# A transformer block in float32: the MLP's down projection from seven block products instead of eight, tokens in two blocks of 1024

## The chip, the cores and the metric

One core of one Trainium2 chip runs the kernel. Its engines have queues of their own: TensorE (PE, with its weight loads shown apart as PEld), VectorE (DVE), ScalarE (ACT), GpSimd (POOL) and SyncE (SP), which here issues nearly all DMAs. TensorE writes its results to PSUM, from where another engine has to fetch them. The metric is the device time of one execution in microseconds. Before the change it is 1821.71 us, the median of 3 runs (1820.71 to 1821.91).

## The reference

```python
x = A_x                                         # 1 x 2048 x 576
mod = (silu(c) @ w_mod).reshape(1, 6, 1, -1)    # sa, ca, ga, sb, cb, gb
h = layernorm(x) * (1 + ca) + sa
x = x + ga * attention(h, wqkv, wo)             # 32 heads, window 256
h = layernorm(x) * (1 + cb) + sb
# block B on h:
g  = gelu(layernorm(h) @ w1)                    # four column groups shifted
x1 = h + shift(g) @ w2                          # by +1, -1, +2, -2 tokens
h2 = gelu(layernorm(x1) @ w3) @ w4              # w3: 576 x 4608, w4: 4608 x 576
x = x + gb * (x1 + h2)
```

All inputs and outputs are float32. The change is in the line of `h2`, the MLP: an up projection to 4608 features, gelu, and a down projection back to 576.

## The kernel before

Matrix products run in a reduced float32 format of TensorE. To keep precision, each operand is split into a high part (a copy rounded to that format, by ScalarE) and a low part (the rest, a subtraction on VectorE or GpSimd), and a product is the sum of three: high by high, high by low, low by high. `products` lists the 14 matmuls of a contraction over 576 (four chunks of 128 rows with three products each, and the 64 rows left over with their low parts stacked into two).

Phase A computes the attention, and phase B the layer norms and the first half of block B (w1, gelu, shifts, w2). Phase B leaves the transposed, split, normalised activations `LNT[g]` for four groups of 512 tokens, and writes `x1` (`accd`) and the residual `x` (`xp`) to DRAM.

Phase C is the MLP. It goes over 18 groups `fg` of 256 hidden features (`NF` = 2 chunks of 128), and within each over 4 token groups `tt` of 512. `up(fg, tt)` makes for each chunk a PSUM tile of 128 features by 512 tokens from 14 matmuls (L1111), applies gelu on ScalarE (L1115, into `gf`), and splits it into `Gc`: the high part on ScalarE (L1117), the low part on VectorE (L1118). `down(fg, tt)` makes for each of 4 token tiles and each half `hf` of 288 output columns a PSUM tile from 2 chunks x 3 = 6 matmuls (L1136) and adds it on VectorE to an accumulator in SBUF (L1140, L1138 for the first group). The 16 accumulators of 128 x 576 stay in SBUF through all 18 groups. The down projection of a unit comes one unit after its up projection.

`weights(fg)` loads two chunks of w3 and two of w4, multiplies w4 by `gb` on GpSimd (L1085), and splits both; the low parts are made on GpSimd, for the first group on VectorE (L857 and L858 for w3, L94 for w4). Raw rows go through a ring of 6 buffers (`row`), split weights through a ring of 9 (`wc`). Once per token tile, between groups 1 and 8, GpSimd computes `x1 * gb + x` and adds it to the accumulator (L1146 to L1148). In the last group each finished accumulator goes to the output by a DMA of 128 x 576.

The order: each step is an event with a time, and `play` runs the events in order of time, which gives the order of the source. In phase A all compute engines keep this order. In phases B and C a scheduler may move instructions on each engine, also across the border between the phases; so weight splits of phase C stand among the last instructions of phase B on GpSimd. PSUM holds, in these phases, tags `w1` (3 tiles, the up projection), `w2` and `tr` (2 each, the down projection) and `mm` (1).

## Time and profile before

| | |
|---|---|
| median of 3 runs | 1821.71 us |
| the profiled execution | 1821.39 us, span 1819.6 us, granted TensorE clock 0.991 |
| PE busy | 1745.1 us (96%) |
| DVE, ACT, POOL busy | 909.8, 631.9, 515.9 us |
| first and last start of an up matmul (L1111) | 892.6 and 1806.0 us |
| first and last start of a down matmul (L1136) | 909.5 and 1815.7 us |
| matmuls of the up and the down projection | 2016 of 128 x 512, 3456 of 128 x 288 |

The page of the profile gives each engine's busy time, the chain of work that ended last, followed back from the last instruction, and groups of instructions. Other views give the durations of the instructions of a line, the instructions in order of time, and busy times in chosen stretches. L12 is line 12 of the kernel before. Matmuls are pipelined: the ends of single ones are modelled, and the spacing of their starts is the better measure.

### The profile page before, as it was taken

To read this page: it belongs to the slowest core of one execution; us is meant where nothing else is said; L and a number is where in the kernel's file an instruction comes from. 1 tells how busy PE (TensorE), PEld (TensorE's weight loads), DVE (VectorE), ACT (ScalarE), POOL (GpSimd) and SP (SyncE) were. 2 spreads that over 40 slices of the span, in tenths; PEclk is the share of its full clock that TensorE was granted. 3 is DMA by queue.
4 is the path that set the end of the run, shared out by engine and by line. 5 is a ranking of instruction groups with operands and counts; after the bars stand their busy time and mean duration, and the time that the engine had idled before them with its cause. 6 is when DMAs were issued, how large, how long until landed. Compare 5 with 4: busy or idle time off the path is not lost.

```text
span 1819.6 us, 30069 instructions
## 1 busy us (share of the span) xinstructions
PE 1745.1 (96%) x11520; PEld 1488.1 (82%) x11520; DVE 909.8 (50%) x2467; ACT 631.9 (35%) x1169; POOL 515.9 (28%) x559
## 2 busy tenths in 40 slices
PE   8899999999998897999899999999999999999999
PEld 5767677777766674888899999999999999999998
DVE  4565665565565763667634443344443333443334
ACT  3354454454455554433222222222222222222211
POOL 7333332321134543112414432343312211221100
PEclk9999999999999998999999999999999999999999
DMA  7554453344356654433301110111101000110002
GB/s 212 163 159 144 122 163 119 114 130 115 89 139 184 194 173 133 143 105 109 123 16 54 47 50 26 54 54 54 53 17 42 26 24 22 28 28 7 1 1 105
DMA packets 128119, 161.18 MB, mean 89 GB/s; under 512 B 35044, under 2 KB 69860, under 8 KB 127976
## 3 DMA queue, kind: packets, MB, share of 16 engines
q1 hardware_dynamic: 127656, 158.74, 29.7%
q8 instruction: 91, 1.49, 0.3%
q10 hardware_dynamic: 320, 0.52, 0.1%
q14 instruction: 52, 0.43, 0.1%
HBM read 107.81 MB, written 50.73 MB: 87 GB/s over the span
## 4 chain that ended last, share of the span: by engine, by line
PE 82%; DVE 5%; POOL 4%; DMA 4%; ACT 2%; issue 2%; SPq 1%; ACTq 0%; POOLq 0%; DVEq 0%
PE p L1136 25%; PE p L1111 25%; PE qk L363 5%; PE av L532 4%; PE X L502 4%; PE sc L455 4%; PE v L363 2%; PE X L511 2%; PE pg L983 2%; PE po L750 2%; PE w L1034 2%; DMA wm<-in_w_mod_dram 1%; DVE sc L462 1%; POOL wm L581 1%; PE oT L543 1%
## 5 line engine op out<-in xcount | busy, mean ns | idle before, releaser
L1111 PE MATMUL p<-LNT,W 128*128 128x512 f32 x2016 | 482.8, 390 | 0.0
L1136 PEld LDWEIGHTS p<-W,Gc 128*128 128x128 f32 x3456 | 472.7, 188 | 11.1
L1136 PE MATMUL p<-W,Gc 128*128 128x288 f32 x3456 | 480.4, 295 | 0.0
L1111 PEld LDWEIGHTS p<-LNT,W 128*128 128x128 f32 x2016 | 371.5, 188 | 69.2
L462 DVE CUSTOM_DVE_ANT_0 sc<-sc,mask 128x384 f32<-128x384 f32 (+2 forms) x512 | 271.2, 541 | 201.1 <-PE sc L455 198.5
L1115 ACT ACTIVATE gfc<-p 128x512 f32<-128x512 f32 x144 | 86.0, 597 | 662.6 <-PE p L1111 662.6
L1140 DVE TENSOR_TENSOR accA<-p,accA 128x288 f32<-128x288 f32 x340 | 151.6, 453 | 316.8 <-PE p L1136 314.9
L521 ACT ACTIVATE P<-X 128x512 f32<-128x512 f32 (+2 forms) x384 | 216.7, 570 | 232.6 <-PE X L511 226.9
L455 PE MATMUL sc<-K,Q 108*128 108x384 f32 (+2 forms) x512 | 191.7, 382 | 5.8 <-DMA k0d<-qe 3.3
L1140 DVE TENSOR_TENSOR accB<-p,accB 128x288 f32<-128x288 f32 x204 | 92.5, 455 | 198.0 <-PE p L1136 196.1
L94 POOL TENSOR_TENSOR W<-r,W 128x576 fp32r<-128x576 f32 x34 | 48.6, 1429 | 466.0 <-ACT W L93 465.9
L502 PE MATMUL X<-Q,K 110*128 110x128 f32 (+2 forms) x704 | 163.0, 306 | 3.7 <-ACT P L521 3.4
L363 PE MATMUL qk<-hT,Wc 128*128 128x512 f32 x504 | 159.4, 414 | 3.6 <-ACT qe L384 1.4
L502 PEld LDWEIGHTS X<-Q,K 110*128 110x128 f32 x704 | 123.9, 191 | 28.7 <-issue 9.4
L1118 DVE TENSOR_TENSOR Gc<-gfc,Gc 128x512 fp32r<-128x512 f32 x144 | 117.5, 816 | 7.7 <-ACT Gc L1117 3.9
L511 PE MATMUL X<-maskb,identb 128*128 128x256 bf16 (+1 forms) x640 | 120.6, 254 | 0.0
L455 PEld LDWEIGHTS sc<-K,Q 108*128 108x128 f32 x512 | 97.5, 193 | 27.8 <-issue 11.7
L363 PEld LDWEIGHTS qk<-hT,Wc 128*128 128x128 f32 x504 | 86.2, 192 | 19.0 <-issue 5.1
L532 PE MATMUL av<-P,V 128*32 128x384 f32 (+2 forms) x1408 | 99.6, 394 | 0.0
L388 POOL CAST qe<-qe 128x512 fp32r<-128x512 f32 x36 | 22.2, 616 | 256.3 <-ACT qe L384 241.2
L1117 ACT CAST Gc<-gfc 128x512 fp32r<-128x512 f32 x144 | 89.3, 620 | 3.6
L363 PE MATMUL v<-Wv,hT 128*128 128x288 f32 x448 | 82.4, 306 | 3.8 <-ACT qe L384 2.9
(891 smaller groups left out, 1842.4 us busy)
## 6 DMA issues: line engine op xcount, KB each, us to landing
K<-k0d SPq DMA_DIRECT2D x96, 108.0 KB
r<-in_B_w_dram SPq DMA_DIRECT2D x36, 288.0 KB
Q<-q0d SPq DMA_DIRECT2D x128, 72.0 KB
K<-k1d SPq DMA_DIRECT2D x48, 108.0 KB
wm<-in_w_mod_dram SPq DMA_DIRECT2D x17, 288.0 KB
x<-in_A_x_dram SPq DMA_DIRECT2D x16, 288.0 KB
Q<-q1d SPq DMA_DIRECT2D x64, 72.0 KB
od<-o SPq DMA_DIRECT2D x32, 144.0 KB
```

Source lines behind the costliest of these rows:

```text
L363: nc.tensor.matmul(pm, pl()[i][0], pl()[i][1], start=(i == 0), stop=(i == 13))
L455: nc.tensor.matmul(sc[:, lo:], q[0:2 * R3, h, i * P:(i + 1) * P], k[0:2 * R3, h // 2, i * P + lo:(i + 3) * P], start=True, stop=True)
L462: nc.vector.tensor_tensor_reduce(out=sc[:, lo:], in0=sc[:, lo:], in1=mask[:, lo:], scale=1.0, scalar=-3e38, op0=ALU.add, op1=ALU.max, accu ...
L502: nc.tensor.matmul(x[:, p0 * P:(p0 + w) * P], k[0:2 * R3 + 2, h // 2, (kb + 2) * P:(kb + 3) * P], q[0:2 * R3 + 2, h, q0 * P:(q0 + w) * P], ...
L511: nc.tensor.matmul(x[:, p0 * P:(p0 + w) * P], self.identb, m, start=False, stop=(n == len(ms) - 1))
L521: nc.scalar.activation(pt[:, c0:c1, h % 2, :], x[:, c0 * P:c1 * P].rearrange("p (a b) -> p a b", b=P), AF.Exp, scale=SCALE)
L532: nc.tensor.matmul(abox[0][32 * h:32 * h + 32, q0 * P:(q0 + w) * P], v[:, hh * VA:hh * VA + 32], Pt[b, h // 2][:, p0:p0 + w, h % 2, :], st ...
L1111: nc.tensor.matmul(pg, w, a, start=(i == 0), stop=(i == len(pl) - 1))
L1117: nc.scalar.copy(Gh, gf)
L1118: nc.vector.tensor_tensor(out=Gl, in0=gf, in1=Gh.bitcast(F32), op=ALU.subtract)
L1136: nc.tensor.matmul(po, a, w, start=(i == 0), stop=(i == len(seq) - 1))
L1140: nc.vector.tensor_tensor(out=acc[t][:, cs], in0=po, in1=acc[t][:, cs], op=ALU.add)
```

## The change

The down projection of a unit is seen as a product of 2 x 2 blocks: 1024 tokens in two halves of 512 (`tt`), 256 features in two chunks of 128 (`j`), 576 columns in two halves of 288 (`DH2`). It is computed from seven products of blocks instead of eight (Winograd's form of Strassen's scheme): combinations of blocks of the gelu output and combinations of blocks of w4 are multiplied, and the products are kept in seven accumulators per token tile, which are combined after the last group.

- Tokens go in two blocks `blk` of 1024, so all of w3 and w4 is needed twice. In block 0 the weights are loaded, combined and split as before, and the split tiles are stored to DRAM (`w3d`, `w4d`); in block 1 they are loaded from there.
- A unit has 4 PSUM tiles of the up projection (14 matmuls of 512 columns each), and 7 products `m` for 4 token tiles `i` of 3 matmuls of 288 columns each. The matmuls of the up projection are issued in pairs between the products of the unit before.
- Four combinations of gelu outputs per unit (128 x 512) and, in block 0, four of w4 blocks (128 x 288) are made on GpSimd. Seven tiles per unit are split instead of four. w4 is multiplied by `gb` on VectorE.
- Each product is added on VectorE to its accumulator: 28 evictions of 128 x 288 per unit.
- The last unit of block 1 is computed plainly with eight products, into accumulators combined one unit earlier; the last unit of block 0 is followed by its combinations, on VectorE and GpSimd, and output goes out in pieces of 128 x 288.
- The residual work (`extra`) is done for one token tile in every second unit.
- All of phase C keeps source order on PE, DVE, ACT and POOL. DMAs on SP are still placed by the scheduler. Weights of the first unit are partly made in phase B, as before.

```diff
+        self.w3d = [[self.dr.tile([P, 2 * KC + 2, P], F32, name=f"w3d{n}_{j}") for j in range(2)] for n in range(F // P // 2)]
+        self.w4d = [[self.dr.tile([P, 2, 2, DH2], F32, name=f"w4d{n}_{j}") for j in range(4)] for n in range(F // P // 2)]
...
-            play(self.phase_c(self.pool(st, "c")))
+            ev = self.phase_c(self.pool(st, "c"))
+            with self.tc.manual_schedule(engines={mybir.EngineType.PE, mybir.EngineType.DVE, mybir.EngineType.Activation, mybir.EngineType.Pool}):
+                play(ev)
...
+    def weights(self, blk, fg):
...
+        l = (nc.gpsimd if fg else nc.vector).tensor_tensor
+        prod = {1: (0, 0), 7: (1, 0), 4: (1, 1), 5: (2, 0), 6: (2, 1), 2: (3, 0), 3: (3, 1), 8: (0, 1)}
...
+        def up(j):
...
+                if blk:
+                    nc.sync.dma_start(w.bitcast(F32), self.w3d[fg][j])
...
+            def lo():
+                w, raw = w3[j], fs[j]
+                l(out=w[:, KC:2 * KC, :], in0=raw[:, 0:KC, :], in1=w[:, 0:KC, :].bitcast(F32), op=ALU.subtract)
+                l(out=w[:, 2 * KC + 1, :], in0=raw[:, KC, :], in1=w[:, 2 * KC, :].bitcast(F32), op=ALU.subtract)
+                nc.sync.dma_start(self.w3d[fg][j], w.bitcast(F32))
...
+        def scale(j):
+            return lambda: nc.vector.tensor_tensor(out=r[j], in0=r[j], in1=self.gb, op=ALU.mult)
+
+        def comb(n):
...
+                (b11, b12), (b21, b22), (t1, t2), (t3, t4) = (half(t) for t in r + c)
+                o, x, y = ((t1, b12, b11), (t3, b22, b12), (t2, b22, t1), (t4, b21, t2))[n]
+                nc.gpsimd.tensor_tensor(out=o, in0=x, in1=y, op=ALU.subtract)
...
+            def lo():
+                w = box["w"]
+                l(out=w[:, 0:m, 1, :], in0=box["s"], in1=w[:, 0:m, 0, :].bitcast(F32), op=ALU.subtract)
+                nc.sync.dma_start(self.w4d[fg][n][:, 0:m], w[:, 0:m].bitcast(F32))
...
+        e = [] if blk else [(0.42, load), (0.7, scale(0)), (0.74, scale(1))] + [(t, comb(n)) for n, t in enumerate((0.75, 0.78, 0.86, 0.92))]
+        for j, t in ((0, 0.85 if (blk, fg) == (1, 1) else 0.6), (1, 0.88)):
+            f, hi, lo = up(j)
+            e += [(t, f)] if blk else [(t, f), (t + 0.001, hi), (t + 0.05, lo)]
+        for n, t in enumerate((1.205, 1.245, 1.305, 1.365)):
+            f, hi, lo = down(n)
+            e += [(t, f)] if blk else [(t, f), (t + 0.001, hi), (t + 0.035, lo)]
...
+        def up(blk, fg, t0):
...
+                    if m == 3:
+                        G3 = self.gp.tile([P, 2 * KC + 1, P], F32R, tag="oT", name=f"G3{nm}", bufs=1)
...
+                        T = cp.tile([P, 2, 512], F32R, tag="G", name=f"G{m}{nm}", bufs=6)
+                    sp[m] = T
+                    nc.scalar.copy(T[:, 0], src())
+
+                def lo():
+                    nc.vector.tensor_tensor(out=sp[m][:, 1], in0=src(), in1=sp[m][:, 0].bitcast(F32), op=sub)
...
+            def comb(o, a, b, op):
+                def f():
+                    nc.gpsimd.tensor_tensor(out=g[o] if o in g else gt(o), in0=g[a], in1=g[b], op=op)
+                return f
...
+                if n == 2:
+                    return [(t + 0.045, comb(4, 0, 2, sub))] + split(7, src(4), t + 0.13, 0.05)
+                e = split(4, src(3), t + 0.03) + [(t + d, comb(*x)) for d, x in ((0.045, (2, 2, 3, add)), (0.1, (0, 2, 0, sub)), (0.155, (1, 1, 0, sub)))]
...
+                t = t0 + 0.25 * n
+                ev += spread([part(2 * k, 2 * k + 2) for k in range(7)], t, t + 0.25)
+                ev += [(t + 0.255, gelu)] + after(n, t + 0.25)
...
+        def extra(blk, n, t0):
...
+            fs = [mul, add] + [into(*x) for x in (((4, 0, ALU.add), (4, 1, ALU.subtract), (7, 1, ALU.add)) if h else ((3, 1, ALU.add), (2, 0, ALU.add)))]
+            return [(t0, load)] + list(zip((t0 + d for d in (0.2, 0.26, 0.4, 0.43, 0.46)), fs))
...
+                    po = box[m, i] = ps.tile([P, DH2], F32, tag=("w2", "tr")[next(cnt) % 2], name=f"p4{nm}_{m}_{i}", bufs=2)
+                    for n, (a, b) in enumerate(seq):
+                        nc.tensor.matmul(po, a, b, start=(n == 0), stop=(n == len(seq) - 1))
...
+                        nc.vector.tensor_tensor(out=acc[m, i], in0=po, in1=acc[m, i], op=ALU.add)
+                    return fin(m, i)
...
+            ms = (2, 4, 5, 3) if plain else (1, 2, 7, 6, 5, 4, 3) if last else (1, 2, 7, 4, 5, 6, 3)
+            e = []
+            for n, (m, i) in enumerate((m, i) for m in ms for i in range(4)):
+                t = t0 + 0.005 + 0.965 * (n + 0.5) / 28
+                f, ev = one(m, i)
+                e += [(t, f), (t + 0.012, ev)]
```

A time of 1 in these events is one unit. `up` of a unit runs from n to n + 1, its `down` from n + 1, and `weights` of it are shifted by n - 1.

More of the change, by code (lines that the diff above doesn't have):

```diff
@@ L30 @@
 R3 = 3 * DH
+DH2 = D // 2
 SCALE = DH ** -0.5
@@ L46, in play @@
         f = heapq.heappop(heap)[2]
-        for t, e in f() or ():
+        r = f()
+        for t, e in r if isinstance(r, list) else ():
             heapq.heappush(heap, (t, n, e))
@@ L1093, in phase_c @@
         nc = self.nc
[L1094 to L1095 removed]
+        NFG = F // P // 2
         ps = self.ps
         gb = self.gb
[L1098 to L1121 removed]
@@ L1154, in phase_c @@
-        units = [(fg, tt) for fg in range(NFG) for tt in range(4)]
-        ev = []
-        for i in range(len(units) + 1):
-            t0 = 0.7 * i
-            if i < len(units):
-                ev += [(t0 + 0.7 * n / NF, f) for n, f in enumerate(up(*units[i]))]
-                if units[i][1] == 1 and units[i][0] + 1 < NFG:
-                    ev.append((t0, lambda fg=units[i][0] + 1: self.weights(fg)))
-            if i >= 1:
-                ev += spread(down(*units[i - 1]), t0, t0 + 0.7)
+        accB = cp.tile([P, 8, DH2], F32, name="accB")
@@ new lines, in phase_c @@
+        units = [(blk, fg) for blk in range(2) for fg in range(NFG)]
+        ev = []
+        for n in range(len(units) + 1):
+            if n < len(units):
+                ev += up(*units[n], n)
+                ev += [(n + t - 1, f) for t, f in (self.weights(*units[n]) if n else self.w0)]
+            if n >= 1:
+                blk, fg = units[n - 1]
+                ev += down(blk, fg, n)
+                if fg % 2 == 0 and fg:
+                    ev += extra(blk, fg // 2 - 1, n + 0.2)
```

223 lines of the change are left out of this document (150 added, 73 removed).

## The prediction

> **What bounds the kernel now.** I read the engines' sums first, then the chain that ended last, then slices of the MLP stage, and last single instructions. Busy time by engine and the chain's shares by line:
>
> ```profile
> PE 1745.1 (96%) x11520; PEld 1488.1 (82%) x11520; DVE 909.8 (50%) x2467; ACT 631.9 (35%) x1169; POOL 515.9 (28%) x559
> PE p L1136 25%; PE p L1111 25%; PE qk L363 5%; PE av L532 4%; PE X L502 4%; PE sc L455 4%; PE v L363 2%; PE X L511 2%; PE pg L983 2%; PE po L750 2%; PE w L1034 2%; DMA wm<-in_w_mod_dram 1%; DVE sc L462 1%; POOL wm L581 1%; PE oT L543 1%
> ```
>
> Half of the chain is the up projection (L1111) and the down projection (L1136) of the MLP. Stretches of that stage, with busy time of PE, PEld, DVE, ACT, POOL, then granted clock and DMA:
>
> ```profile
> 900.00:910.00 10.00, 9.55 (x40) 8.09 (x41) 2.95 (x6) 3.50 (x7) 5.80 (x4) 0.83 0.28 84
> 1000.00:1100.00 100.00, 100.00 (x598) 91.18 (x597) 40.11 (x79) 23.18 (x42) 37.18 (x28) 1.00 0.18 49
> 1500.00:1600.00 100.00, 100.00 (x601) 91.38 (x601) 39.57 (x79) 24.39 (x44) 19.61 (x16) 1.00 0.08 23
> ```
>
> TensorE never pauses there and runs at full clock; DVE is 40% busy, POOL at most 37%. So time saved on PE is time saved, until another engine fills. The chain's pieces in order of time (start, length, what):
>
> ```profile
> 549.65 6.70 DMA K<-k1d
> 901.75 7.90 PE p L1111 x31
> 1001.86 3.18 PE p L1111 x14
> 1008.22 3.18 PE p L1111 x14
> 1806.40 9.56 PE p L1136 x72
> ```
>
> Fourteen up matmuls take 3.18 us, 0.227 each. From one such group to the next are 6.36 us, so the 24 down matmuls between take 3.18 too, 0.1325 each; 72 in a row cost 9.56/72 = 0.133, so changing between the two kinds costs nothing visible.
>
> **PE.** Call 1024 tokens by 256 hidden features a unit: 36 units. Before, a unit is 56 up and 96 down matmuls: 4 x 6.36 = 25.44 us. After, seven products x 4 token tiles x 3 split terms = 84 down matmuls: 12.72 + 11.13 = 23.85 us. The last unit keeps the plain eight products (96). Removed: 35 x 12 = 420 matmuls x 0.1325 = 55.65 us, all of it on the chain. In source order PE alternates two up matmuls (0.454) with one product (0.398), so a product appears every 0.85 us; four PSUM buffers let PE run 3.4 us ahead of a late eviction.
>
> **What the other engines get.** Durations (min/median/max ns) in the MLP stage:
>
> ```profile
> L1140 DVE TENSOR_TENSOR accA<-p,accA x324: 439/456/461, 980.4 to 1796.9; 128x288 f32<-128x288 f32 x162
> L1118 DVE TENSOR_TENSOR Gc<-gfc,Gc x140: 681/692/1971, 911.0 to 1795.0; 128x512 fp32r<-128x512 f32 x140
> L857 POOL TENSOR_TENSOR W<-W_1r,W x16: 1280/1298/1736, 942.7 to 1705.9; 128x512 fp32r<-128x512 f32 x16
> L858 POOL TENSOR_TENSOR W<-W_1r,W x16: 451/920/930, 943.9 to 1707.1; 128x128 fp32r<-128x128 f32 x16
> L94 POOL TENSOR_TENSOR W<-r,W x32: 1427/1430/1437, 936.4 to 1721.0; 128x576 fp32r<-128x576 f32 x32
> L1117 ACT CAST Gc<-gfc x140: 620/620/626, 910.3 to 1794.3; 128x512 fp32r<-128x512 f32 x140
> L1115 ACT ACTIVATE gfc<-p x140: 597/597/598, 909.7 to 1793.7; 128x512 f32<-128x512 f32 x140
> L93 ACT CAST W<-r x32: 667/670/677, 935.6 to 1720.2; 128x576 fp32r<-128x576 f32 x32
> ```
>
> POOL per unit of the first token block: four combinations of gelu outputs (4 x 1.29), four of w4 blocks (288 columns: between 0.45 and 1.29, by slope 0.80; 3.2), low parts of w3 (2 x 1.74) and of w4 (0.80 + 3 x 1.43): 16.9 us. Every second unit adds the residual work ("extra"): 2 x 1.43 and two, later three, 0.80 adds, 4.5 then 5.3 us. DVE: 28 evictions x 0.456 = 12.8, seven low splits instead of four, and in block 0 two 576-wide scalings (0.75, the slope of L1118's 0.69). ACT: 4 x 0.60 + 7 x 0.62 + at most eight weight casts of 0.67 = 12.1 of 23.85: hidden beside PE. In block 1 the split weights come back by DMA and POOL keeps 5.2 + 5.3 us: nothing fills there, DVE 12.8 + 7 x 0.69 to 0.85 = 18 to 19 us.
>
> Evictions stay at 439 to 461 ns whatever POOL does; L1118, with both inputs in SBUF, ranges to 1971. Start, length, instruction around two such cases:
>
> ```profile
> 1038.12 1.43 POOL L94 TENSOR_TENSOR W<-r,W 128x576 fp32r<-128x576 f32 x1 [7.77 <-ACT W L93]
> 1038.84 1.26 DVE L1118 TENSOR_TENSOR Gc<-gfc,Gc 128x512 fp32r<-128x512 f32 x1
> 1039.58 0.34 SPq L1084 DMA_DIRECT2D r<-in_B_w_dram  x1
> 1042.51 1.42 POOL L1085 TENSOR_TENSOR r<-r,gb 128x576 f32<-128x576 f32 x1 [2.96 <-DMA r<-in_B_w_dram]
> 1044.43 1.30 POOL L857 TENSOR_TENSOR W<-W_1r,W 128x512 fp32r<-128x512 f32 x1 [0.49 <-ACT W L852]
> 1045.20 1.07 DVE L1118 TENSOR_TENSOR Gc<-gfc,Gc 128x512 fp32r<-128x512 f32 x1
> 1045.67 0.92 POOL L858 TENSOR_TENSOR W<-W_1r,W 128x128 fp32r<-128x128 f32 x1
> 1050.88 0.69 DVE L1118 TENSOR_TENSOR Gc<-gfc,Gc 128x512 fp32r<-128x512 f32 x1
> ```
>
> The split begun at 1038.84 ends 0.55 after POOL's instruction, that of 1045.20 0.54 after; alone it takes 0.69. The POOL instruction behind it, 0.45 alone, takes 0.92 and ends 0.32 after DVE: it lost 0.40 from 1045.73. So a split costs POOL 0.40 us, and DVE up to a POOL instruction plus 0.55. Per pair of units (one with extra) POOL needs 2 x 16.9 + 4.5 to 5.3 + 14 x 0.40 + 4 x 0.46 = 45.7 to 46.5 us against PE's 47.7. It fits, barely. But DVE works in source order: behind a split or scaling that waits for POOL, a cast or a DMA stand evictions, and behind those PE, once its 3.4 us are used up.
>
> The Trainium skill ("SBUF — State Buffer", "SBUF: two separate sides") calls this pair of ports an exclusive lock held for the whole instruction. By that rule each split blocks POOL for its full 0.69, a pair needs 51 to 52 us, and block 0 would lose some 5 us more than I take. The trace agrees on the lock, but shows 0.40.
>
> **Block 0, three units followed by hand** (us from a unit's start; eviction k is available at 0.85(k+1)). A unit without extra, POOL free at 0.65: three gelu combinations, each letting one split in, then w4's four low parts from 5.3 to 11.6; the latest eviction, number 9, starts 1.8 late: no PE stall. w3's low part waits for its cast at 13.8; scaling 17.5 to 19.7, w4 combinations and the seventh product's G until 23.4, the last w3 part until 25.6, 1.1 later than POOL was free before. The next, with extra: low parts end at 12.8; eviction 7 ends 3.4 late, so products 11 and 13 stall PE 0.5; extra until 18; the scaling waits for that and for its rows (issued about 14.2, landing 2.93 later as 1039.58 to 1042.51, behind one store); POOL ends 3.4 into the third. There evictions 4, 5, 7 and 9 come too late for products 8, 9, 11, 13: 0.1 + 1.0 + 1.0 + 0.1. By then PE has slipped 2.2, and POOL is on time again. Per pair 2.7 us, and 3.5 where extra has 5.3: 4 x 2.7 + 4 x 3.5 = 25 us. This is my least certain term: 0 if the slack takes it, 57 in the slow case below. I stay at 25, since it follows DVE and POOL instruction by instruction.
>
> **The ends.** The hand-over from the stage before:
>
> ```profile
> 893.32 0.21 DVE L105 BATCH_NORM_AGGREGATE d15mv<-d15st 128x2 f32<-128x12 f32 x1
> 897.36 0.21 POOL L110 TENSOR_SCALAR d15rs<-d15mv 128x1 f32<-128x1 f32 x1
> 898.57 1.73 DVE L133 TENSOR_SCALAR xm<-x,d15mv,d15rs 128x576 f32<-128x576 f32 x1
> 900.45 1.09 PE L71 MATMUL LT15pa<-ident,xm 128*128 128x128 f32 x4 [5.05 <-DVE xm L133]
> ```
>
> POOL reads d15mv 3.8 us late because weight splits stand ahead of it; L133 is stretched too; PE idles 5.05, and the next 31 up matmuls take 7.90 instead of 31 x 0.227 = 7.04. In the new order of POOL nothing stands between d14 and d15: about 5 of these 5.9 us go, 5.5 with the clock; 0.8 of idle may remain, so between 3 and 6. The first unit has no down work to hide behind, and weights of the second must be made in 12.7 us instead of 23.85: 2 us (0 to 5). At the block change and in the unit before the last, 8 and 12 DVE adds of 288 (0.39 alone, about 0.79 with POOL) raise DVE to 12.8 + 7 + 6.3 = 26.1 and about 25.9: 2 us each, 4 (0 to 8).
>
> **DMA.** SP gets six stores a unit in block 0 (3.4 MB, the loads 1.2 MB): 193 GB/s. The nearest rows, the first 40 us in slices of 1 us, with rows of 4.6 KB:
>
> ```profile
> GB/s 0 39 244 127 237 191 270 396 406 415 419 424 424 223 197 262 264 246 152 212 220 369 300 198 141 260 325 224 253 106 13 186 121 217 63 257 49 0 0 148
> wm<-in_w_mod_dram SPq DMA_DIRECT2D x4, 576.0 KB
> ```
>
> At 400 a 590 KB store takes 1.5 us, about POOL's time to make it: hidden, at 0 cost, unless loads behind stores land late.
>
> **The sum**, against the profiled execution's 1821.39 (0.3 under the median of 1821.71): 1821.39 - 55.65 - 5.5 + 2 + 25 + 4 = 1791.2.
>
> **Rivals.** (1) PE stays dense: slack takes the stalls. 1821.39 - 55.65 - 5.5 + 3 = 1763. For it: 47.7 against 46. Against: evictions and splits stand in one queue, and POOL is idle while it waits for rows. Chance 0.2. (2) Mine, 1780 to 1803: 0.5. (3) Between, 1803 to 1818, stalls of 37 to 52 us as rows land later in units with extra: 0.14. (4) Slower. The rows of the next weights reuse buffers that w4's last low part frees, and their loads stand behind its store on SP. The ring is: last low part, load, scaling, four combinations (3.2) and one of gelu (1.3), w3's low part (1.75), three gelu combinations (3.9), four low parts (5.1), six splits (2.4), scalings (1.4): 19 us plus issue 1.5 plus landing. With 2.93 it is 23.4, under 23.85; with the 6.70 of the longest landing on the chain it is 27.2. All 17 units at that pace lose 57 us: 1821.39 - 55.65 - 5.5 + 6 + 57 = 1823, and it decides above about 6.5 us in every unit. Against it: half the units load two low parts earlier. Idle gaps also cost clock (900 to 910: 0.83, 0.86 us for 31 matmuls): 17 such gaps would make it 1838. The Trainium skill ("TensorE: Matmul & The Clock Gate", "What's actually happening") drops the clock to half after one idle window of about 3.4 us; the 0.83 after 5.05 us agrees in kind. Chance 0.14. (5) No change, 1818 to 1825: 0.02. That the products are not saved can't be: the matmuls are counted.
>
> **Numbers.** 1791; likeliest case 1780 to 1803; 8 in 10: 1768 to 1818, leaving out most of (4), (5) and the lower part of (1). Measurable is about 0.2% (3.6 us): faster 0.84, same 0.02, slower 0.14.
>
> **What would show it.** 3036 down matmuls, still near 0.1325 in dense stretches; units of block 1 at 23.85, of block 0 near 25.3 on average, alternating; DVE above 85% and POOL near 90% busy in block 0; PE idle released by DVE evictions (PSUM), not by DMA; the splits' mean in block 0 near 1.1 us. LT15's transposes start near 895.5. Wrong if block 1 is slower than 24.5 a unit, or scalings wait for DMA in every unit of block 0.

## The result and the profile after

The changed kernel takes 1794.0 us (median of four runs, 1793.53 to 1795.58), the kernel before 1821.2: a ratio of 0.985, with a 95% interval of 0.984 to 0.987. That is 27 us less; 1791 was forecast, with 1768 to 1818 as the range. The profiled execution took 1793.53 us, its span is 1791.7.

Busy time by engine, from the page of the changed kernel:

```profile
PE 1712.6 (96%) x11100; PEld 1431.1 (80%) x11100; DVE 1227.2 (68%) x3050; ACT 713.7 (40%) x1310; POOL 839.5 (47%) x829
```

420 matmuls fewer (11520 to 11100), DVE from 50% to 68%, POOL from 28% to 47%. Now the same kind of stretches of the MLP stage as before (busy time of PE, PEld, DVE, ACT, POOL, then granted clock, DMA share, GB/s); the first lies in the first token block ("block 0"), the second runs over the change of blocks, the third lies in block 1:

```profile
1000.00:1100.00 100.00, 98.02 (x561) 85.59 (x560) 78.92 (x148) 40.86 (x76) 86.38 (x73) 1.00 0.59 198
1345.00:1355.00 10.00, 8.33 (x31) 7.10 (x32) 5.82 (x12) 0.60 (x1) 9.29 (x12) 0.66 0.31 110
1500.00:1600.00 100.00, 100.00 (x579) 88.98 (x578) 73.50 (x145) 26.55 (x44) 35.20 (x24) 1.00 0.46 152
```

In block 1 TensorE stays busy at full clock. In block 0 it pauses a little, with POOL at 86% and DVE at 79%. At the change of blocks it pauses, and the clock drops to 0.66.

The start of a unit can be read from TensorE's own rows: the last two up matmuls of a unit and the first two of the next stand together, a group of four (start, length, instruction):

```profile
1324.72 1.09 PE L1231 MATMUL p<-LNT,W 128*128 128x512 f32 x4
1357.11 1.09 PE L1231 MATMUL p<-LNT,W 128*128 128x512 f32 x4
1381.36 1.09 PE L1231 MATMUL p<-LNT,W 128*128 128x512 f32 x4
```

From 1357.11 to 1381.36 are 24.25 us, and so it goes on to the end of block 1: the dense unit is 24.25 and not 23.85. The unit before took 32.39. The chain within a dense unit (start, length, what):

```profile
1441.26 0.47 PE p L1231 x2
1441.73 0.40 PE p L1276 x3
1442.13 0.47 PE p L1231 x2
```

Two up matmuls and one product come every 0.866 us (1442.13 - 1441.26, over many rows), where 2 x 0.227 + 3 x 0.1325 = 0.852 was counted.

For all comparisons below I cut each profile at two marks on TensorE: A, the first transposes after attention (xnT0pa), and B, the transposes of the last token tile (LT15pa), with which the MLP stage begins to run on its own. Times in us; "MLP" is from B to the end of the span. Ratios are to the kernel before, with 95% intervals.

| kernel | median | ratio | A at | A to B | MLP |
|---|---|---|---|---|---|
| before | 1821.2 | 1 | 713.9 | 186.5 | 919.2 |
| changed | 1794.0 | 0.985 (0.984 to 0.987) | 709.3 | 178.5 | 903.9 |
| changed, again | 1795.9 | 0.986 (0.983 to 0.988) | 715.0 | 179.1 | 901.2 |
| order alone, eight products | 1830.2 | 1.006 (1.004 to 1.008) | 709.1 | 178.5 | 937.0 |
| seven products, scheduler's order | 1896.7 | 1.042 (1.041 to 1.044) | 712.4 | 183.8 | 998.2 |
| groups of four and two | 1783.6 | 0.980 (0.978 to 0.982) | 714.8 | 179.2 | 891.7 |
| groups of eight and four | 1791.5 | 0.984 (0.982 to 0.987) | 710.6 | 179.3 | 899.1 |
| no residual work in block 0 | 1785.1 | 0.980 (0.978 to 0.983) | 711.2 | 178.9 | 890.9 |
| its loads only | 1785.8 | 0.980 (0.978 to 0.982) | 712.1 | 178.1 | 892.6 |
| its GpSimd work only | 1803.3 | 0.990 (0.987 to 0.992) | 713.2 | 178.5 | 911.3 |
| last combinations spread | 1787.3 | 0.981 (0.979 to 0.984) | 713.7 | 179.2 | 895.1 |
| four and two, and spread | 1774.2 | 0.975 (0.973 to 0.977) | 711.9 | 179.1 | 881.0 |
| same, residual on VectorE | 1774.2 | 0.975 (0.973 to 0.976) | 712.6 | 179.1 | 881.6 |
| same, earlier in its order | 1775.9 | 0.976 (0.974 to 0.977) | 708.5 | 179.2 | 886.2 |

The profiles' difference of 27.9 us (span 1819.6 to 1791.7) thus has three parts: 4.6 up to A, 8.0 from A to B, 15.3 in the MLP stage.

### The profile page after: what moved, and what is told of

Read it like the earlier page. It is cut to its first block, busy times and chain, and to the rows that moved or that the text cites. A ratio compares the mean times of both kernels' runs of the same rounds, so it can differ in the third digit from the quotient of the medians.

```text
span 1791.7 us, 31913 instructions
## 1 busy us (share of the span) xinstructions
PE 1712.6 (96%) x11100; PEld 1431.1 (80%) x11100; DVE 1227.2 (68%) x3050; ACT 713.7 (40%) x1310; POOL 839.5 (47%) x829
## 4 chain that ended last, share of the span: by engine, by line
PE 75%; DVE 7%; POOL 6%; DMA 5%; issue 4%; ACT 2%; SPq 1%; DVEq 0%; POOLq 0%; ACTq 0%
PE p L1231 21%; PE p L1276 19%; PE qk L365 6%; PE av L534 4%; PE X L504 4%; PE sc L457 4%; PE v L365 3%; PE X L513 3%; PE w L1037 2%; PE pg L986 2%; PE po L752 2%; DMA r<-in_B_w_dram 1%; POOL g L1204 1%; POOL c L1132 1%; DMA wm<-in_w_mod_dram 1%
## 5 line engine op out<-in xcount | busy, mean ns | idle before, releaser
L1231 PE MATMUL p<-LNT,W 128*128 128x512 f32 x2016 | 628.7, 399 | 0.0
L1276 PEld LDWEIGHTS p<-W,G 128*128 128x128 f32 x3036 | 505.2, 189 | 116.7 <-DVE accA L1283 14.7
L1276 PE MATMUL p<-W,G 128*128 128x288 f32 x3036 | 559.9, 296 | 16.7 <-DVE accA L1283 7.7
L1283 DVE TENSOR_TENSOR accA<-p,accA 128x288 f32<-128x288 f32 x672 | 293.1, 453 | 134.9 <-PE p L1276 131.9
L1231 PEld LDWEIGHTS p<-LNT,W 128*128 128x128 f32 x2016 | 327.4, 188 | 5.4
L1204 POOL TENSOR_TENSOR g<-g,g 128x512 f32<-128x512 f32 x140 | 204.9, 1463 | 245.6 <-ACT g L1235 240.3
L1199 DVE TENSOR_TENSOR G<-g,G 128x512 fp32r<-128x512 f32 x249 | 247.1, 992 | 28.2 <-ACT G L1196 27.7
L1196 ACT CAST G<-g 128x512 fp32r<-128x512 f32 x249 | 154.7, 621 | 225.5 <-POOL g L1204 222.0
L1235 ACT ACTIVATE g<-p 128x512 f32<-128x512 f32 x144 | 85.7, 595 | 360.3 <-DVE accA L1283 211.3
L1283 DVE TENSOR_TENSOR accB<-p,accB 128x288 f32<-128x288 f32 x268 | 114.0, 448 | 26.9 <-PE p L1276 24.9
L457 PEld LDWEIGHTS sc<-K,Q 108*128 108x128 f32 x512 | 96.9, 192 | 28.5 <-issue 11.8
L365 PEld LDWEIGHTS qk<-hT,Wc 128*128 128x128 f32 x504 | 87.7, 194 | 17.6 <-issue 5.1
```

What stands on the lines that cost most here:

```text
L365: nc.tensor.matmul(pm, pl()[i][0], pl()[i][1], start=(i == 0), stop=(i == 13))
L457: nc.tensor.matmul(sc[:, lo:], q[0:2 * R3, h, i * P:(i + 1) * P], k[0:2 * R3, h // 2, i * P + lo:(i + 3) * P], start=True, stop=True)
L1199: nc.vector.tensor_tensor(out=sp[m][:, 1], in0=src(), in1=sp[m][:, 0].bitcast(F32), op=sub)
L1204: nc.gpsimd.tensor_tensor(out=g[o] if o in g else gt(o), in0=g[a], in1=g[b], op=op)
L1231: nc.tensor.matmul(box["p"], box["l"][i][1], box["l"][i][0], start=(i == 0), stop=(i == 13))
L1276: nc.tensor.matmul(po, a, b, start=(n == 0), stop=(n == len(seq) - 1))
```

## The experiments

**Does the change between the two kinds of matmul cost something?** The prediction read from the profile before, where 14 up matmuls stand together, that it does not. Now there are 27 changes of each direction in a unit. Groups of four up matmuls and two products halve them:

```diff
-                ev += spread([part(2 * k, 2 * k + 2) for k in range(7)], t, t + 0.25)
+                ev += [(t0 + ((7 * n + k) // 2 * 2 + 0.5 + 0.01 * ((7 * n + k) % 2)) / 28, part(2 * k, 2 * k + 2)) for k in range(7)]
...
-                t = t0 + 0.005 + 0.965 * (n + 0.5) / 28
+                t = t0 + 0.005 + 0.965 * (n // 2 * 2 + 1.0 + 0.01 * (n % 2)) / 28
```

> The changed kernel with TensorE's order made coarser: four up matmuls and then two products (six down matmuls), where the changed kernel has two and one. All other work is the same. Theory (each change between the two kinds of matmul costs some 7 ns, 0.40 us over the 28 pairs of changes of a unit): a unit of the second token block takes 24.05 us instead of 24.25, and the kernel some 7 us less, 1787 us. Rival A (the cost sits in each product of three short matmuls, not in the change): units stay at 24.25 and the time at 1794. Rival B (coarser groups use up the four PSUM buffers sooner): units of the first token block get longer than 49.9 us a pair, and the kernel is no faster or slower, 1794 to 1805.

The chain in block 1, with these groups:

```profile
1442.97 0.91 PE p L1231 x4
1443.88 0.80 PE p L1276 x6
1444.68 0.92 PE p L1231 x4
```

1444.68 - 1442.97 = 1.71 us for what two rounds of 0.866 = 1.732 did. From one unit to the next, here at a group of eight:

```profile
1377.78 1.99 PE L1231 MATMUL p<-LNT,W 128*128 128x512 f32 x8
1401.74 1.99 PE L1231 MATMUL p<-LNT,W 128*128 128x512 f32 x8
```

That is 23.96 us, where 24.05 was expected. The MLP stage shrinks by 12.2 us (903.9 to 891.7): 16 units of block 1 give 16 x 0.29 = 4.6, the 15 units of block 0 give 374.72 - 366.76 = 8.0, of which 4.4 is the same and 3.6 are stalls; the other units lose 0.4. Rival A and rival B fall. Once more, eight and four:

```diff
-                ev += spread([part(2 * k, 2 * k + 2) for k in range(7)], t, t + 0.25)
+                ev += [(t0 + ((7 * n + k) // 4 * 4 + 0.5 + 0.01 * ((7 * n + k) % 4)) / 28, part(2 * k, 2 * k + 2)) for k in range(7)]
...
-                t = t0 + 0.005 + 0.965 * (n + 0.5) / 28
+                t = t0 + 0.005 + 0.965 * (n // 4 * 4 + 2.0 + 0.01 * (n % 4)) / 28
```

> The changed kernel with groups of eight up matmuls and four products on TensorE. The run with groups of four and two took a unit of the second token block from 24.25 us to 23.96. Theory (13 to 16 ns for each pair of changes): halving the changes again brings the unit to some 23.88. Rival (four products in a row want four PSUM buffers at once, and the gelu's tiles arrive late): the dense units get no shorter than 23.96, and the first token block stalls more than the 7.4 us of the run with groups of two: no faster than that run from the last tile's transposes to the end, 891.7 us.

The chain in block 1:

```profile
1576.90 1.82 PE p L1231 x8
1578.72 1.58 PE p L1276 x12
1580.30 1.82 PE p L1231 x8
```

A round of eight and four takes 3.40 us, 0.850 per product: seven rounds are 23.80 us a unit, less than the 23.88 expected. Theory and rival were each right in part. The matmuls cost what was counted when the groups are long, but in block 0 TensorE now waits 11.7 us for evictions in DVE's hands, and the stage takes 899.1 us. Per product the three orders cost 0.866, 0.856 and 0.850 us: 16, 6 and 0 ns above the last. What in TensorE takes the 16 ns was not tried.

**What stalls block 0?** First the place. Counted from 0, the units 3, 5, ... 17 of block 0 have residual work. POOL, DVE, TensorE, and what they wait for, in the unit after one with residual work, in the changed kernel:

```profile
978.60 4.36 POOL L1204 TENSOR_TENSOR g<-g,g 128x512 f32<-128x512 f32 x3
982.10 1.41 DVE L1199 TENSOR_TENSOR G<-g,G 128x512 fp32r<-128x512 f32 x1
983.43 0.81 DVE L1283 TENSOR_TENSOR accB<-p,accB 128x288 f32<-128x288 f32 x2
983.93 0.66 PE L1276 MATMUL p<-W,G 128*128 128x288 f32 x3 [0.56 <-DVE accB L1283]
```

A split that begins during a POOL instruction takes 1.41 us, where it takes 0.69 alone; it ends 0.55 after that instruction. It stands in front of two evictions, and the product behind them starts 0.56 late. In a unit with residual work the place is another (SPq is the DMA queue):

```profile
965.26 1.84 SPq L1102 DMA_DIRECT2D r<-in_B_w_dram  x2
970.01 0.76 DVE L1123 TENSOR_TENSOR r<-r,gb 128x576 f32<-128x576 f32 x1 [2.04 <-DMA r<-in_B_w_dram]
972.69 0.67 PE L1276 MATMUL p<-W,G 128*128 128x288 f32 x3 [0.36 <-DVE accA L1283]
```

Here a scaling waits 2.04 us for rows of w4, which SP issued 14.8 us after the unit's first up matmul (950.47), and the evictions that TensorE needs stand behind it and the second scaling. The two places cost the same: from first up matmul to first up matmul, the eight units with residual work lose 5.5 us over 24.25 each, and the seven between them 5.5.

To see whether the residual work ("extra") is what makes POOL late, it was split into its two halves; but first it was left out in block 0:

```diff
-                if fg % 2 == 0 and fg:
+                if blk and fg % 2 == 0 and fg:
```

Its loads only:

```diff
-            return [(t0, load)] + list(zip((t0 + d for d in (0.2, 0.26, 0.4, 0.43, 0.46)), fs))
+            return [(t0, load)] + list(zip((t0 + d for d in (0.2, 0.26, 0.4, 0.43, 0.46)), fs)) * blk
```

Its GpSimd work only:

```diff
-                nc.sync.dma_start(r[0], self.accd[t])
-                nc.sync.dma_start(r[1], self.xp[t])
+                if blk:
+                    nc.sync.dma_start(r[0], self.accd[t])
+                    nc.sync.dma_start(r[1], self.xp[t])
...
-                nc.gpsimd.tensor_tensor(out=r[0], in0=r[0], in1=gb, op=ALU.mult)
+                nc.gpsimd.tensor_tensor(out=r[0], in0=r[0] if blk else gb, in1=gb, op=ALU.mult)
...
-                nc.gpsimd.tensor_tensor(out=r[0], in0=r[0], in1=r[1], op=ALU.add)
+                nc.gpsimd.tensor_tensor(out=r[0], in0=r[0], in1=r[1] if blk else gb, op=ALU.add)
```

> The changed kernel without the residual work of the first token block (the eight groups of two loads, a multiplication, an addition and two or three adds on GpSimd); the residual is then missing from the first 1024 tokens of the output. Theory (the stalls of the first token block come from GpSimd, which has 43 of a pair's 49.9 us to do and is late in the unit after such a group): a pair of units falls from 49.4 to 50.5 us to 48.5, some 11 us less in all, about 1783 us. Rival (the splits wait for the weights' rows, which land too late, whatever GpSimd does): pairs stay at 49.9, the kernel loses at most 2 us.

> The changed kernel, with the residual work of the first token block cut to its loads: both rows of each group are still fetched into their buffers, but GpSimd's multiplication, addition and adds into the accumulators are left out there, so the residual is missing from the first 1024 tokens. Without the whole residual work the first block had no stall (15 units in 363.7 us), with it 11.0 (374.7). Theory A (GpSimd's 4.5 to 5.3 us per group cause them): 363.7 to 365. Theory B (the two rows more in the ring of six row buffers, and their traffic, make the next weights' rows late): 372 to 375.

> The counterpart: the residual work of the first token block keeps GpSimd's instructions and the row buffers, but fetches nothing (it multiplies and adds a row of constants that lies in SBUF already, so the residual of the first 1024 tokens is a wrong value). Theory A (GpSimd's time): 15 units of the first block in 373 to 375 us. Theory B (traffic and landing): 363.7 to 366. In between: both, by the share that is left.

The same 15 units of block 0 in the four kernels, each in a stretch from the start of unit 3 to that of unit 18 (the first unit is 0): length, then busy time of PE, PEld, DVE, ACT, POOL. In the changed kernel:

```profile
950.00:1324.72 374.72, 368.00 (x2102) 321.75 (x2101) 298.87 (x553) 151.65 (x281) 324.93 (x271) 1.00 0.59 202
```

Without the residual work:

```profile
952.31:1316.00 363.69, 363.69 (x2102) 323.63 (x2101) 295.79 (x553) 152.23 (x281) 284.42 (x235) 1.00 0.59 196
```

With its loads only:

```profile
952.27:1315.97 363.70, 363.70 (x2102) 323.64 (x2101) 295.69 (x553) 152.23 (x281) 284.41 (x235) 1.00 0.62 209
```

With its GpSimd work only:

```profile
953.86:1336.94 383.08, 368.78 (x2102) 321.62 (x2101) 300.04 (x553) 151.74 (x281) 322.05 (x271) 1.00 0.53 186
```

15 dense units are 15 x 24.25 = 363.7. Without the residual work nothing is lost, and its loads alone lose nothing either: the stalls, 11.0 us, come with POOL's instructions of the residual work, 40 us of its time (324.93 - 284.42). That holds for both places. Without the residual work no scaling waits for its rows, which are issued 7.7 to 8.0 us after a unit's first up matmul; with its loads only they are issued 7.7 to 11.8 us after it, and in the changed kernel, in the units with residual work, 14.1 to 16.1. The loads stand in SP's order behind stores of split weights that wait for POOL, which fits; but with the loads only, the residual's row buffers also come free as soon as the rows have landed, so POOL's time isn't told from the time for which these rows hold their buffers.

The kernel without the fetches did worse than the changed kernel, 19.3 us of stalls, which neither theory expected. The units between lose 5.6 us, as before; those with residual work lose 13.8. There the rows of w4 are issued 17.0 to 17.6 us after a unit's first up matmul, the DVE scalings wait 23.6 us for them where the changed kernel's wait 11.2, and weight casts wait 26 us for rows of w3. Dropping the fetches also changed when the row buffers become free and what SP issues when, so it is no clean half. It shows that POOL's work is enough for stalls without the traffic; why SP issued the rows later still stays open.

**The two ends of the blocks.** At the end of block 0 each finished tile is combined by DVE and POOL adds that the changed kernel puts right behind the evictions. In the changed kernel, at the change of blocks (DVE and TensorE) and in the unit before the last:

```profile
1345.84 0.94 DVE L1289 TENSOR_TENSOR accA<-accA 128x288 f32<-128x288 f32 x1
1346.70 0.68 DVE L1199 TENSOR_TENSOR G<-g,G 128x512 fp32r<-128x512 f32 x1
1347.80 1.09 PE L1276 MATMUL p<-W,G 128*128 128x288 f32 x3 [1.63 <-DVE accA L1283]
...
1771.89 0.67 PE L1276 MATMUL p<-W,G 128*128 128x288 f32 x3 [2.51 <-DVE accA L1283]
```

The adds take 0.46 us alone and 0.94 beside POOL's, and they stand in one queue with the evictions. Putting them off and spreading them:

```diff
+                def out(m):
+                    t = 8 * blk + i + 4 * (m > 3)
+                    d = DH2 * (m in (3, 5))
+                    nc.sync.dma_start(self.out[t * P:(t + 1) * P, d:d + DH2], A(m))
...
-                        va(6, 6, 1)
-                        va(7, 7, 6)
-                        va(6, 6, 5)
-                        pa(4, 4, 7)
-                        pa(5, 5, 7)
-                    elif m == 3:
-                        return [(0.0, lambda: pa(3, 3, 6))]
+                        return [(t0 + 0.86 + 0.02 * i, lambda: va(6, 6, 1)), (t0 + 1.0 + 0.03 * i, lambda: va(7, 7, 6)), (t0 + 1.12 + 0.03 * i, lambda: va(6, 6, 5)),
+                                (t0 + 1.02 + 0.03 * i, lambda: pa(4, 4, 7)), (t0 + 1.22 + 0.02 * i, lambda: pa(5, 5, 7)), (t0 + 1.3 + 0.02 * i, lambda: pa(3, 3, 6))]
...
-                    if m == 1:
-                        pa(2, 2, 1)
-                    elif m == 6:
-                        va(6, 6, 1)
...
+                    if m == 6:
+                        return [(t0 + 0.62 + 0.06 * i, lambda: va(6, 6, 1)), (t0 + 0.65 + 0.06 * i, lambda: va(7, 7, 6))]
+                    late = {2: (0.3 + 0.03 * i, (2, 2, 1)), 4: (0.87 + 0.02 * i, (4, 4, 7)), 5: (0.95 + 0.02 * i, (5, 7, 5)), 3: (1.17 + 0.02 * i, (3, 3, 6))}
...
```

> The changed kernel with the last combinations of the block products put off and spread: at the change of token block and in the unit before the last, the adds of finished accumulators on VectorE and GpSimd come after the gelu combinations and one at a time between evictions, and the output's stores after them. Nothing is left out. Theory (the 8.1 us lost in the two units around the change of block, the 4.5 lost in the unit before the last and the 1.7 of lower clock at the end come from these adds in a burst): 8 to 13 us less, 1781 to 1786 us; the two units take about 50 us instead of 56.6, the unit before the last about 25 instead of 28.7. Rival (the change of block costs what it does because the first weights of the second block wait for their loads and the gelu combinations for GpSimd anyway): less than 3 us less.

Starts of the same units as above, with the adds spread:

```profile
1331.59 1.09 PE L1231 MATMUL p<-LNT,W 128*128 128x512 f32 x4
1355.84 1.09 PE L1231 MATMUL p<-LNT,W 128*128 128x512 f32 x4
1381.95 1.08 PE L1231 MATMUL p<-LNT,W 128*128 128x512 f32 x4
```

24.25 and 26.11 us, 50.36 where the changed kernel takes 56.64 (1324.72 to 1381.36): 6.3 less. The unit before the last falls from 28.9 to 24.7, which is a dense one by this count: 4.2 less (the last 96 matmuls start at 1773.95, 28.89 after their unit's start, and now at 1770.37, 24.72 after it). These 96 now run at full clock, 1.7 us less, but 1.6 are lost again between them, and this execution's block 0 took 1.7 more. The MLP stage is 8.8 us shorter, as the theory had it; the medians differ by 6.7, short of the 8 expected.

**The order by itself, and the products by themselves.** Order alone, as an edit of the kernel before:

```diff
-            play(self.phase_c(self.pool(st, "c")))
+            ev = self.phase_c(self.pool(st, "c"))
+            with self.tc.manual_schedule(engines={mybir.EngineType.PE, mybir.EngineType.DVE, mybir.EngineType.Activation, mybir.EngineType.Pool}):
+                play(ev)
```

Seven products in the scheduler's order, as an edit of the changed kernel:

```diff
-            with self.tc.manual_schedule(engines={mybir.EngineType.PE, mybir.EngineType.DVE, mybir.EngineType.Activation, mybir.EngineType.Pool}):
-                play(ev)
+            play(ev)
```

> The kernel before, with eight products, with the one edit that all engines keep source order in the MLP stage. Theory (source order brings 5 us at the hand-over from the stage before, since GpSimd no longer reads the last token tile's statistics behind weight splits; the rest of the gain is the seventh product): the last tile's transposes start about 5 us earlier against the up matmuls behind them, the kernel takes 1814 to 1818 us, against 1821. Rival (the 7.4 us by which the changed kernel reaches the MLP stage early are brought by the order too): 1807 to 1811. Rival (the order written out is worse than the scheduler's within the stage): 1825 or more.

> The changed kernel, seven products and all, but with the order of the MLP stage left to the scheduler again, as in the kernel before. Theory (source order is needed for seven products: with the scheduler's order PE is held by late evictions behind splits, and the hand-over's idle comes back): from the last tile's transposes to the end it takes more than the changed kernel's 903.9 us, by 5 to 30 us, and the hand-over loses 5 to 8; the kernel takes 1805 to 1830. Rival (the product alone carries the gain, and the scheduler orders it as well as the source does): 1790 to 1800, the hand-over's 8 us lost again.

Order alone brings the whole gain from A to B: 178.5 us, as in the changed kernel, against 186.5. But its MLP stage is 17.8 us longer than before, and the kernel is slower by 0.6%, as the last of the rivals had it. A stretch of it, and pieces of its chain:

```profile
1500.00:1600.00 100.00, 98.39 (x588) 89.32 (x587) 34.32 (x76) 24.86 (x44) 18.02 (x16) 1.00 0.09 26
```

```profile
1008.51 1.40 POOL r L1087
1009.91 0.02 issue
1009.94 0.02 ACT W L93
1009.96 0.56 issue
1010.51 0.60 ACT gfc L1117
...
1012.59 0.46 DVE accB L1142
1013.05 0.14 issue
1013.18 3.42 PE p L1138 x24
```

A gelu stands in ACT's order behind a weight cast that waits for POOL's multiplication, and DVE's split and eviction stand behind the gelu. TensorE loses 1.6 us per 100, some 15 of the 17.8.

Seven products in the scheduler's order are far worse than I thought, 94 us in the MLP stage where 5 to 30 were expected. A stretch of its block 0, then DVE and TensorE in it:

```profile
1000.00:1100.00 100.00, 86.86 (x478) 71.67 (x477) 69.18 (x125) 35.29 (x66) 70.73 (x60) 1.00 0.50 171
```

```profile
1100.43 0.76 DVE L1122 TENSOR_TENSOR r<-r,gb 128x576 f32<-128x576 f32 x1 [3.80 <-DMA r<-in_B_w_dram]
1101.11 0.45 DVE L1282 TENSOR_TENSOR accA<-p,accA 128x288 f32<-128x288 f32 x1
1101.61 0.67 PE L1275 MATMUL p<-W,G 128*128 128x288 f32 x3 [1.75 <-DVE accA L1282]
```

DVE waits 3.80 us for rows of w4 with an eviction behind the scaling, and TensorE waits for the eviction. Over the run, DVE's splits also wait far longer for their casts (us in total, times, longest), here and then in the changed kernel:

```profile
DVE G L1198 <- ACT G L1195: 101.8, 91, 8.6
```

```profile
DVE G L1199 <- ACT G L1196: 25.6, 21, 3.4
```

Rows that land late are rival (4)'s mechanism, but over the run DVE waits 33.6 us for them (11.2 in the changed kernel), and 101.8 for the casts. How the 94 us divide between the two was not separated. The hand-over loses 5.3 us, as expected (183.8 from A to B). So neither half is a gain alone: the order costs 17.8 us in the MLP stage with eight products, and with seven it is worth 94.

**Is the earlier end of attention an effect of the change?** Up to A all kernels issue the same instructions in the same order on TensorE. The changed kernel was run once more, unchanged.

> The changed kernel once more, unchanged, for the stages ahead of the MLP, whose instructions stand in the same order in all kernels shown. Theory (the end of the attention stage differs from execution to execution by some microseconds, 709.1 to 714.8 in the profiles so far, so 4.6 us of the two profiles' difference is no effect of the change): it again lies anywhere in that range, the stretch from there to the last tile's transposes takes 178 to 179.5 us, and the MLP stage 902 to 906. Rival (the change moves that end): 709.3 again within 0.5 us.

Range and median length (ns) of the four transposes at A, and first and last start, in the changed kernel, then in its second profile:

```profile
L73 PE MATMUL xnT0pa<-ident,xn x4: 272/273/299, 709.3 to 709.6; 128*128 128x128 f32 x4
```

```profile
L73 PE MATMUL xnT0pa<-ident,xn x4: 421/421/447, 715.0 to 715.7; 128*128 128x128 f32 x4
```

The same kernel reaches A at 709.3 and at 715.0, the latter 0.2 beyond the range expected. The 4.6 us by which the first profile was ahead there lie within what executions of one kernel differ by, and what A to B and the MLP stage show (179.1 and 901.2, the latter just under the range expected) holds without them.

**A version that beats both.** The two edits that gained, together:

> The two edits that gained, together: groups of four up matmuls and two products, and the last combinations put off and spread. Theory (the two gains lie in different places, so they add: 12.1 and 8.8 us from the last tile's transposes to the end, of 903.9): that stretch takes 882 to 886 us, the kernel 1772 to 1779. Rival (with the longer groups the spread adds stand in front of evictions that TensorE needs sooner): less than 5 us better than the coarser order alone, 1779 to 1784.

1774.2 us, a ratio of 0.975 (0.973 to 0.977), and 881.0 us in the MLP stage: 22.9 us under the changed kernel, where the two gains sum to 21.0 (882 to 886 was expected). They add up. What is left in block 0 are 6.7 us of stalls (366.06 for 15 units of 23.96), 5.3 of them in the units with residual work. I tried to take them by moving the residual's multiplication and addition to DVE, then by moving these two earlier in DVE's order:

```diff
-                nc.gpsimd.tensor_tensor(out=r[0], in0=r[0], in1=gb, op=ALU.mult)
+                (nc.gpsimd if blk else nc.vector).tensor_tensor(out=r[0], in0=r[0], in1=gb, op=ALU.mult)
...
-                nc.gpsimd.tensor_tensor(out=r[0], in0=r[0], in1=r[1], op=ALU.add)
+                (nc.gpsimd if blk else nc.vector).tensor_tensor(out=r[0], in0=r[0], in1=r[1], op=ALU.add)
...
-            return [(t0, load)] + list(zip((t0 + d for d in (0.2, 0.26, 0.4, 0.43, 0.46)), fs))
+            ds = (0.2, 0.26, 0.4, 0.43, 0.46) if blk else (0.3, 0.34, 0.35, 0.38, 0.41)
+            return [(t0, load)] + list(zip((t0 + d for d in ds), fs))
```

And the second, as an edit of the first:

```diff
-            ds = (0.2, 0.26, 0.4, 0.43, 0.46) if blk else (0.3, 0.34, 0.35, 0.38, 0.41)
+            ds = (0.2, 0.26, 0.4, 0.43, 0.46) if blk else (0.14, 0.18, 0.35, 0.38, 0.41)
```

> Both edits, and the residual work's multiplication and addition of the first token block moved from GpSimd to VectorE (GpSimd keeps the two or three adds into the accumulators), in the middle of the unit. Theory (GpSimd's load of a pair decides the stalls of the first block, the whole of which went when the residual work was left out): of the 7.4 us that the first block loses with the coarser order, 4 to 7 go, 877 to 882 us from the last tile's transposes to the end. Rival (VectorE in source order now waits for the residual's rows, or shuts GpSimd out longer): the stalls stay or grow, no better than both edits alone.

> As the kernel with the residual's multiplication and addition on VectorE, but these two stand 0.16 of a unit (3.8 us) earlier in VectorE's order. There GpSimd worked 20 us less in the first token block, but stood 25.6 us in front of its adds, waiting for VectorE's result (3.2 us in each of the eight groups), and the block's 15 units took 366.7 us, as without the move. Theory (that wait ate the gain): the wait goes, the 15 units take 360 to 363 us, the stretch from the last tile's transposes to the end 874 to 879 us, the kernel 1767 to 1772. Rival (VectorE, in source order, is late itself in the unit after a group, whoever does the residual work): 366 to 367 again, 881 us and 1774.

POOL's adds into the accumulators in block 0, with the idle time before them and what ended it, in the first of the two:

```profile
L1258 POOL TENSOR_TENSOR accA<-accA,ex 128x288 f32<-128x288 f32 x16 | 15.8, 999 | 26.0 <-DVE ex L1255 25.6
```

And in the second:

```profile
L1258 POOL TENSOR_TENSOR accA<-accA,ex 128x288 f32<-128x288 f32 x16 | 14.2, 900 | 18.8 <-DVE accA L1284 12.5 <-DVE ex L1255 5.9
```

POOL has 20 us less to do but stands 25.6 us waiting for DVE's result; 366.68 us for the 15 units, no gain, which was the rival. Earlier in DVE's order, that wait falls to 5.9, but POOL then waits 12.5 for evictions, and the 15 units take 371.33. Both theories of that last run missed: it was worse than either. What the rest of the stalls hangs on stays open.

## Why the prediction was right, and where it was not

The forecast was 3 us from the measured time and the likeliest case was the right one, but several terms were off and cancelled. That it came so near is luck: the 14 us that the forecast had too much for block 0 are the 14 that it lacked for the changes between the kinds of matmul, and 4.6 us of the two profiles' difference come before A, where TensorE's instructions are the same in both kernels.

**PE, -55.65.** The 420 matmuls are gone, and all of it was on the chain. "Changing between the two kinds costs nothing visible" was the failed step: it was read from groups of 14 up matmuls, and applied to groups of two. It costs 0.40 us a unit, 35 x 0.40 = 14 us that stood nowhere in the sum. The runs with longer groups show that it belongs to the changes (24.25, 23.96, 23.80 us a unit).

**The hand-over, -5.5.** Right. The statistics of the last tile, and its transposes, in the changed kernel:

```profile
886.15 0.22 POOL L112 TENSOR_SCALAR d15rs<-d15mv 128x1 f32<-128x1 f32 x1 [3.38 <-DVE d15mv L107]
887.13 0.57 DVE L135 TENSOR_SCALAR xm<-x,d15mv,d15rs 128x576 f32<-128x576 f32 x1
887.85 0.63 PE L73 MATMUL LT15pa<-ident,xm 128*128 128x128 f32 x4 [0.38 <-DVE xm L135]
```

POOL takes them up 0.1 us after DVE ends them (886.07), not 3.8, and TensorE idles 0.38 instead of 5.05. Order alone gives the same A to B. But the 8.0 us there are 3 more than this idle: the stage ahead also got shorter, which I had not looked for. POOL is busy 22.5 us from A to B, where it was 36.9 with MLP weights in between; that this is the cause was not tried.

**The first unit, +2.** The unit after it, in which its products start, took 27.09 us from its first up matmul to that of the next (899.13 to 926.22), 2.8 over a dense one.

**Block 0, +25.** The cause was right: the stalls are in DVE evictions that stand behind splits and scalings, and without the residual work they are gone. The place was half right: the forecast had 0.5 us in a unit with residual work, at products 11 and 13, and 2.2 in the one after it, behind stretched splits, so that units alternate. Measured are 0.7 in a unit with residual work, late in it and behind scalings that wait for their rows, and 0.8 in the one after it; the units don't alternate. The size was not right: 11.0 us (9.9 in the second profile), 1.4 a pair instead of 2.7 to 3.5. The splits of block 0 and their cost to POOL:

```profile
L1199 DVE TENSOR_TENSOR G<-g,G 128x512 fp32r<-128x512 f32 x98 | 103.9, 1060 | 15.7 <-ACT G L1196 15.1
```

Their mean of 1060 ns is the forecast's 1.1. But POOL is busy 324.93/15 x 2 = 43.3 us a pair, not 45.7 to 46.5: beside the 33.8 of its own work (2 x 16.9) and 4.9 of residual work that leaves 4.6 for 18 splits and scalings, 0.26 each instead of 0.40; not each of them holds a POOL instruction up. And TensorE's own pair is 48.5 us, not 47.7, so POOL's slack is 5.2 us where I had 1.2 to 2.0. The Trainium skill ("SBUF — State Buffer", "SBUF: two separate sides") has a lock held for the whole instruction. The forecast priced that at 51 to 52 us a pair. The trace does not bear the price out, but it says little against the lock: the split of 982.10 above did wait until POOL's instruction ended at 982.96.

**The change of blocks and the unit before the last, +4.** Too small: 8.1 and 4.2 us, and 1.7 for the clock in the last 96 matmuls. I counted the adds' time on DVE over the whole unit, but they come in a burst behind the evictions of m = 6 with four PSUM buffers behind them. Spreading them gave back 6.3 and 4.2.

**The sum** of these for the MLP stage is -55.65 + 14.0 + 2.8 + 11.0 + 8.1 + 4.2 + 1.7, less 1.7 for the slower clock that the last tile's transposes (0.8) and the first up matmuls (0.9) had before: -15.5, and the trace shows -15.3. With 8.0 from A to B that is 23 us, 25 in the second profile. The profiles show 27.9, of which 4.6 come before A; the medians show 27.2. What they have beyond 23 to 25 stays open: there is one profile of the kernel before.

**The rivals.** TensorE dense, 1763: no, though the stalls are nearer to it than to mine. Rows late in every unit, above 1821: not in this order; rows that land late with evictions behind them are a part of what the scheduler's order shows (1896.7). The marks set for "wrong" (block 1 above 24.5 a unit, scalings waiting for DMA in every unit) were not reached: 24.25, and in block 0 six waits with 11.2 us in all, in six of the eight units with residual work. DVE reached 79% in block 0, not 85.

## What to carry to other kernels

A price that a profile shows for long groups of one kind of matmul is not yet the price of short ones: divide a period of the new order, not a run of the old. Where engines work in source order, look at what stands in a burst in front of evictions: spreading 20 short adds on DVE, and POOL's adds and the output's stores with them, gave 8.8 us in the MLP stage and 6.7 by the medians, a quarter to a third of what the whole change gave. And before a difference between two profiles is put down to an edit, see whether a stage that the edit does not touch moved as well; a second profile of the same kernel tells.

## What the runs showed of the hardware

- A product of three 288-column matmuls with its two 512-column matmuls takes 0.866 us where the two kinds alternate in groups of two and three, 0.856 in groups of four and six, 0.850 in groups of eight and twelve.
- The granted clock fell after short idle gaps: to 0.66 in the stretch from 1345 to 1355, after gaps of 0.92 and 1.63 us, and to 0.50 in a stretch of the run with groups of four and two (below) after gaps of 1.76 and 2.11. The Trainium skill ("TensorE: Matmul & The Clock Gate", "What's actually happening") speaks of an idle window of about 3.4 us; no single gap before these two drops was as long.

```profile
1767.18:1772.18 5.00, 5.00 (x23) 5.00 (x23) 2.51 (x6) 0.00 (x0) 2.76 (x4) 0.50 0.17 59
```

- A DVE add of 128x288 with both inputs in SBUF takes 0.46 us and 0.94 beside POOL adds; an eviction from PSUM of the same size stays at 0.45.
- The end of the attention stage, whose instructions are the same on TensorE in all kernels, lay between 708.5 and 715.0 us in 14 profiles, more than most effects looked for here.
